# Gated linear attention and a bilinear feed-forward on one core: chunks 2 to 5 in blocks of 64 tokens, with a new order of the work

## The chip, the core and the metric

The kernel runs on one core of a Trainium2 chip. The core has TensorE (PE, matrix products, written to PSUM), VectorE (DVE), ScalarE (ACT), GpSimd (POOL) and SyncE (SP, which here issues transfers). They run side by side, each through its own list of instructions in order, and wait for one another by semaphores. Times are device microseconds (us) of one execution; the measure is the median of several.

## What is computed

Inputs are q, k, v and alpha, each 4 batches x 8 heads x 768 tokens x 48, in float32. A state of 48 x 48 per batch and head is carried over the tokens; its output y, put together over the heads to 3072 tokens x 384, goes through a feed-forward layer with two branches that are multiplied.

```python
for t in range(S):
    state = alpha[:, :, t, :, None] * state + np.einsum('bhd,bhe->bhde', k[:, :, t], v[:, :, t])
    y[:, :, t] = np.einsum('bhd,bhde->bhe', q[:, :, t], state)
x = y.transpose(0, 2, 1, 3).reshape(B * S, H * D)
out = (x @ w_a) * (x @ w_b) @ w_out          # 384 -> 1536 -> 384
```

## The kernel before, in words

**Chunks.** The work is six chunks. A chunk is 256 tokens of two batches (u = 0 and 1) with all 8 heads; chunks 2s and 2s+1 take the tokens from 256 s on, for batches 0, 1 and 2, 3. Partition p holds tokens 2p and 2p+1 (rank r = 0, 1), so partitions 0 to 63 are the first 128 tokens (frame g = 0) and 64 to 127 the second (g = 1). The state at the start of a chunk is in `S0`, that between its frames in `Sm`.

**What is done to a chunk.** `ln` takes the logarithm of alpha on ScalarE (L548); `l2` adds the pairs (L556); a product with a triangle of ones gives cumulative sums (`A`, `B`, `A2`; `AQ` for chunks 2 to 5, which needs two transfers `sw` that swap the frames' halves, L603, and the splits `R` on VectorE, L614); `E` takes their exponentials both ways on ScalarE (L658), `ra` the exponential of the second rank (L636). `lv`, `mk` and `mq` scale k and q by them (L643, L669) into `QKp`. `C`/`Ce` (TensorE and a copy) or `T` (a transposing transfer on SyncE, L722) turn `QKp` to `kqT`. Then come four kinds of small products on 64x64 quarters of TensorE's array:

- scores `D` (L777): keys by queries, within a frame and for each rank of the key, 64 x 128;
- the state products `K` (L748), 64 rows deep, 48 columns wide, and the update `k` on VectorE (L762 to L766);
- `SB`, `SA` (L801): queries by the state at the frame's start, the part carried in;
- `Y` (L801): masked scores by values, the inner part, into the same PSUM banks.

The scores are masked on VectorE from PSUM (`M`, L782) or copied by ScalarE and masked afterwards (`Mc`, L786, and `Mm`, L790). `v` copies the values into a padded tile (L734, L736). `X` puts the result into `xT` (L836, L838). The feed-forward follows: for each of 12 slices f of the hidden width, `a f` and `b f` (L855) are three products each, over 512 columns (`*`, the whole chunk) or 256 (one u); `as` copies the first branch out on ScalarE (L861), `pr` multiplies it with the second on VectorE (L869); `o m h` (L877) makes an output block of 128 tokens in two halves of six products, `ot` copies it out (L892, L894), `st` stores it.

**The order.** It is written by hand in the string `PROGRAM`: each entry is chunk, operation, arguments, the last of them a PSUM bank (0 to 7) or an engine (V, S, P, Y for VectorE, ScalarE, GpSimd, SyncE). Each engine gets its instructions in just that order, and the feed-forward of one chunk is woven into the attention part of the next. `a 6 * 3` is slice 6 of the first branch for the whole chunk in bank 3. A bank that is written again waits until its last reader is done: for `a`, the `as` on ScalarE; for `b`, the `pr` on VectorE. `dr` and `dl` carry the chunk's decay through memory into `bl`. `c1a` loads ScalarE's function table that has both Ln and Exp:

```python
    def const_table():
        nc.scalar.preload_act_table_set("natural_log_exp_and_others")
```

It is the fifth entry of the string, ahead of all activations.

Of the kernel before, what the change touches and what calls it, by code (L numbers as in the profile page):

```python
# [17 lines left out]
0: cz 0 q V; cs 0 m P; ld a 0b Y; c1; c1a; cs 0 0 P; cz 0 v V; ld a 0a Y; ln 0b; cu; fill 5 2; ld k 0b Y; ld q 0b Y; cu2 P; cus; cm 0; cz 1 q V; B 0b 0; ld q 0a Y  # L18
0: ld v 0 P; ld k 0a Y; ld a 1 P; ln 0a; ld q 1 P; ci; ld k 1 P; E 0b b; B 0a 3; E 0b i; W b 0 256; ld v 1 P; E 0a b; dk 0 0; mq 0b V; mk 0b V; E 0a i; C 0 1 5
0: mq 0a V; mk 0a V; cz 0 b P; fill 3 1; cm 1; Ce 0 1 V; C 0 0 1; W a 0 256; de 0; v 0 V; Ce 0 0 V; D 0 1 6; K 0 0 3; k 0 0 V; SB 0 2; W a 256 768; c3 V  # L20
0: M 0 1; ln 1; D 0 0 0; W b 256 768; Mc 0 0; B 1a 4
1: ld a 1 P
0: E 1a b
1: ld a 0 P
0: Mm 0 0 V; W a 768 1536; cz 1 b P; B 1b 0; E 1a i; E 1b i; cs 1 0 P; mk 1a V; E 1b b; dk 1 5; W b 768 1536; mq 1a V; Y 0; v 1 S; C 1 0 1; mq 1b V; mk 1b V
0: de 1; SA 0; Ce 1 0 V; C 1 1 6; X 0 S; Ce 1 1 V; K 1 0 0; D 1 0 4; a 0 0 3
1: ld k 0 P
0: Mc 1 0
1: ld q 0 P
0: k 1 0 V; D 1 1 1; M 1 1; a 1 0 7  # L30
1: ld v 0 P
0: a 5 0 6
1: ld q 1 P
0: Mm 1 0 V; a 3 0 5; as 1 0; as 0 0; Wo 0 6; b 0 0 7; as 5 0; c2 P; pr 0 0; SB 1 1; b 1 0 0; a 2 0 6; b 2 0 3; a 4 0 4; pr 1 0; as 2 0; b 5 0 0; pr 2 0
0: pr 5 0
1: ld k 1 P
0: as 3 0
1: ln 1
0: SA 1; Y 1
1: l2 1 V  # L40
0: K 1 1 0; K 0 1 3; k 1 1 V; X 1 S; as 4 0; b 4 0 6; b 3 0 5
1: ln 0
0: b 5 1 2; pr 3 0; a 4 1 4; a 5 1 0; a 1 1 7
1: l2 0 V
0: k 0 1 V; as 4 1; pr 4 0; b 1 1 5; as 5 1; b 2 1 1; b 4 1 0; a 6 * 4
1: H 0 S
0: Wo 6 12; as 1 1
1: H 1 S
0: pr 5 1; b 3 1 6; a 3 1 3; pr 4 1; a 11 * 0; a 8 * 2; a 2 1 7; pr 1 1; as 3 1
2: ld a * P  # L50
1: L 1 V; L 0 V
0: pr 3 1; as 6 *; as 8 *
1: ra 0
0: as 2 1; b 6 * 6
1: lv 0 q P
0: pr 6 *; b 8 * 5; b 11 * 4
1: A2 0 7
0: a 7 * 3
1: ld v 1 P
0: as 11 *; a 9 * 6; a 0 1 2  # L60
1: lv 0 k V; E 0 b; ra 1
0: pr 8 *
1: E 0 i
0: pr 2 1; b 9 * 0
1: A2 1 5
0: b 0 1 1; a 10 * 7; as 0 1; pr 11 *; as 9 *
1: E 1 b; mq 0 V
0: as 7 *; cz 1 v P; cs 1 m P
2: ld k * P
0: b 7 * 4; b 10 * 2  # L70
1: E 1 i; mk 0 V; lv 1 q V; C 0 1 6; mq 1 V
0: pr 9 *
1: Ce 0 1 S; C 0 0 3; dk * 0
0: pr 0 1; pr 7 *
2: ld v * P
1: v 0 V; D 0 1 5; K 0 0 1
0: as 10 *
1: K 0 1 4; de *; Ce 0 0 S; Mc 0 1; k 0 0 V
0: o 3 0 7; o 1 0 0; pr 10 *
1: lv 1 k V  # L80
2: ld q * P
1: mk 1 V; k 0 1 V; D 0 0 5; SB 0 1
2: ln *
1: M 0 0
0: o 0 0 3
1: Mm 0 1 V
0: o 0 1 -
1: C 1 1 4; Ce 1 1 V
0: o 3 1 -; ot 0 V
1: v 1 V; C 1 0 4  # L90
0: o 1 1 -
2: lv 0 k P; l2 * V
1: Ce 1 0 S; Y 0; K 1 0 5; K 1 1 6
2: sw Y
1: k 1 0 V; SA 0; D 1 0 3; X 0 S
0: o 2 0 5
1: k 1 1 V
0: ot 3 S; ot 1 V
2: ra 0
1: M 1 0; a 3 0 1; a 1 0 2; as 3 0; as 1 0; b 1 0 0  # L100
2: ra 1
1: a 11 0 7; b 3 0 6
3: ld a * P
1: a 5 0 2
0: o 2 1 -
1: pr 1 0; as 5 0
2: R 0
1: D 1 1 3; pr 3 0
2: lv 1 k P; R 1
0: ot 2 S  # L110
1: b 5 0 2; b 11 0 0; b 4 0 6; pr 5 0; a 4 0 1; Mc 1 1; as 11 0; Mm 1 1 V
2: v 0 V; AQ 4
1: as 4 0; pr 11 0; SB 1 2; a 2 0 1; a 10 0 7
3: ld v * P
4: ld a * P
1: b 10 0 0; pr 4 0
2: E 0 b
1: as 2 0; b 2 0 1; as 10 0
2: lv 1 q V; E 1 b; E 1 i
1: pr 10 0  # L120
2: lv 0 q V
1: SA 1; Y 1
2: E 0 i
1: pr 2 0; X 1 S; a 7 0 7; a 0 0 4; a 6 0 1
2: mk 1 V
1: as 6 0; b 6 0 5
2: dr
1: b 7 0 3
2: mq 1 V
1: as 7 0; a 0 1 2; a 8 0 0; b 0 0 7; pr 6 0; pr 7 0; as 0 0; as 8 0; pr 0 0; b 8 0 6; as 0 1  # L130
3: ln *
1: a 9 0 3
2: T 1
1: pr 8 0; b 0 1 4; pr 0 1; a 5 1 7; a 2 1 0; b 2 1 2
2: mq 0 V; dl
1: a 11 1 5; a 4 1 6; b 8 1 1; as 2 1; as 9 0; as 11 1; b 11 1 4; pr 2 1
2: v 1 V; mk 0 V
1: as 4 1; b 9 0 5
2: T 0
1: pr 9 0; b 4 1 3; a 6 1 6; a 9 1 2; b 9 1 0; as 5 1; b 3 1 5  # L140
0: st 1 Y
1: pr 4 1; pr 11 1
3: l2 * V
1: a 3 1 7; as 9 1; as 3 1
3: ra 0
1: b 5 1 3; pr 5 1; a 1 1 2; b 1 1 4; pr 9 1; a 8 1 7; pr 3 1
2: K * 0 0
1: as 6 1
0: st 0 Y; st 3 Y
3: sw Y  # L150
1: as 1 1; as 8 1
3: ra 1
2: D 1 0 5
0: st 2 Y
2: D 1 1 2
1: pr 1 1
2: M 1 1; Mc 1 0
1: b 6 1 4; pr 6 1; o 2 0 7; a 7 1 6
2: k * 0 V
3: ld k * Y; ld q * Y  # L160
1: a 10 1 2; as 10 1; as 7 1
5: ld k * Y
1: b 7 1 3; b 10 1 5; pr 10 1; o 2 1 -; pr 7 1; pr 8 1
2: Mm 1 0 V; SB 1 5; K * 1 3
4: ln *
1: ot 2 S
2: D 0 0 0
1: o 0 0 4; o 3 0 7
2: k * 1 V; Mc 0 0; SB 0 2
3: R 0; lv 0 q P  # L170
2: D 0 1 0
1: o 3 1 -
2: Y 1
3: R 1
2: Mc 0 1; Mm 0 1 V; Mm 0 0 V
3: lv 0 k V; AQ 0
2: SA 1
3: E 1 b; E 0 i
2: SA 0; Y 0; X 0 S
1: o 0 1 -  # L180
2: X 1 V
3: E 0 b
2: b 6 * 2; a 6 * 3
4: l2 * V
1: ot 0 S
3: E 1 i
2: as 6 *; a 2 * 6; a 1 * 4; b 7 * 5; a 5 * 0
4: sw Y
3: dr
2: b 1 * 3  # L190
3: mk 0 V
1: ot 3 V
2: as 1 *; as 2 *; b 8 * 1; a 8 * 7
3: mq 0 V; lv 1 q P
2: pr 6 *; b 2 * 6
3: lv 1 k P
4: ld q * Y
3: T 0
1: st 3 Y
4: ra 0  # L200
2: as 8 *; pr 1 *
3: mk 1 V
2: as 5 *
3: v 0 S
4: R 0
3: mq 1 V
2: pr 8 *
1: st 2 Y
3: T 1
2: a 7 * 2; pr 2 *; b 3 * 7; a 4 * 3; b 5 * 0; b 9 * 1; as 7 *; b 0 * 4; a 3 * 6; a 9 * 2; pr 7 *  # L210
4: R 1
2: pr 5 *; as 3 *
1: o 1 0 5
3: v 1 V
2: a 0 * 6; as 9 *; as 0 *
3: dl
1: o 1 1 -; st 0 Y
5: ld a * Y
2: pr 9 *; pr 3 *; as 4 *; pr 0 *
1: ot 1 V  # L220
4: ld k * Y
2: b 4 * 6; a 10 * 0
3: K * 0 1
5: ld q * Y
2: pr 4 *
3: D 0 0 4; M 0 0
2: b 10 * 3; a 11 * 6; b 11 * 7; as 10 *
3: k * 0 V
2: o 3 0 4; as 11 *; pr 10 *; pr 11 *
3: D 1 1 0; D 1 0 2; K * 1 5; k * 1 V; Mc 1 0; Mc 1 1  # L230
4: ra 1
2: o 0 0 7; o 0 1 -
3: SB 0 2
2: ot 0 S
3: SB 1 5; D 0 1 0
5: lv 1 k V
3: Mm 1 1 V
5: ln *
2: o 2 0 7
3: M 0 1; Mm 1 0 V  # L240
2: o 2 1 -; ot 2 V
4: AQ 0
3: SA 1
4: lv 1 q P; lv 0 q P; lv 1 k P
3: SA 0; Y 0
# [12 lines left out]
3: a 8 * 5
4: E 0 i; lv 0 k P
3: a 1 * 1; a 5 * 3  # L260
4: mq 0 V
1: st 1 Y
3: as 8 *; as 5 *; a 0 * 7
5: ld v * P; ra 1
3: b 8 * 2; a 9 * 6; a 3 * 3
5: lv 1 q P; lv 0 q V
4: mq 1 V; mk 0 V
3: b 5 * 0; pr 8 *; pr 5 *; b 3 * 5
5: lv 0 k P
3: b 9 * 4; as 9 *  # L270
4: mk 1 V; T 0; dr
3: a 4 * 6; a 2 * 2; as 3 *; as 1 *; b 2 * 1
5: R 0
3: pr 9 *; b 1 * 3
4: T 1
3: b 0 * 4; b 6 * 0
4: v 0 V
3: pr 3 *; pr 1 *; as 2 *
4: dl
2: st 0 Y  # L280
3: pr 2 *; as 4 *; as 0 *
4: v 1 S
3: b 4 * 5
4: D 0 0 2; Mc 0 0
3: a 11 * 1; pr 0 *; pr 4 *; a 6 * 6; as 11 *; a 7 * 7; as 6 *; as 7 *
4: D 1 1 4
3: pr 6 *
5: R 1
4: D 0 1 1; K * 0 3; Mc 0 1; k * 0 V; D 1 0 6; Mc 1 1
3: a 10 * 0; b 11 * 1  # L290
2: o 1 0 2
3: pr 11 *
4: Mm 0 0 V; Mc 1 0
# [72 lines left out]
4: pr 2 *; pr 9 *
3: st 3 Y; st 2 Y; st 1 Y
# [30 lines left out]
def kernel(  # L398
# [443 lines left out]
    def us_of(w):  # L842
        return FULL if w == "*" else HALVES[int(w)]
# [186 lines left out]
```

## Time and profile before

| | |
|---|---|
| Runs, us | 197.16, 196.88, 197.66 (median 197.16) |
| Profiled execution: span, us | 194.9; the page gives no other time of it, 2.3 under the median |
| TensorE busy, us | 188.1 |
| VectorE, ScalarE, GpSimd busy, us | 133.5, 106.7, 48.6 |
| Feed-forward products L855: 324 of 512, 216 of 256 columns, busy us | 81.0, 31.2 |
| Output products L877: 276 of 384 columns, busy us | 49.7 |
| Scores, state, carried and inner products: count | 384, 320, 240, 576 |
| TensorE's granted clock | full in all slices |

Busy times of TensorE overlap, because products are pipelined; the chain of waits in order of time gives the pace. A line of the groups names line, engine, operation, result and sources, shapes and count, then busy time and mean ns, then idle time before and what ended it. A line of the timeline or the chain begins with the start and the duration in us.

### The profile page before, as it was taken

The page shows a single profiled execution, that of the slowest core. Times are in us where ns is not written, and L with a number is a line of the kernel's source. Part 1 is how long each engine was busy: PE and PEld are TensorE (multiplying, and loading weights), DVE is VectorE, ACT ScalarE, POOL GpSimd, SP SyncE. Part 2 cuts the span into 40 slices and gives each one's busy share as a digit, 9 for nine tenths or more (in the row PEclk, how much of TensorE's full clock was granted, in tenths as well). Part 3 has the DMA queues.
Part 4 walks back from the last instruction along what each step waited for, and adds up shares of the span by engine and source line. Part 5 has one row for each costly group of instructions (what it writes and reads, how often), then busy time and mean ns, then how long its engine had stood idle before and what let it go on. Part 6 is the DMA issues. An engine that isn't in the chain of part 4 may idle for free.

```text
span 194.9 us, 6070 instructions
## 1 busy us (share of the span) xinstructions
PE 188.1 (97%) x2612; PEld 117.9 (60%) x2612; DVE 133.5 (69%) x224; ACT 106.7 (55%) x195; POOL 48.6 (25%) x67
## 2 busy tenths in 40 slices
PE   5989999999979999999999999999999999999993
PEld 2887875667658876644466644556455644455662
DVE  4477897986789989889888779689372816432311
ACT  4367677655668676644428655971394443632211
POOL 7999535901900000170005840000000000000000
PEclk9999999999999999999999999999999999999999
DMA  5999999999993799949999697501873100000314
GB/s 137 274 216 227 238 255 232 251 272 240 247 240 90 117 252 266 247 92 268 153 253 257 69 213 150 99 0 45 150 152 119 45 3 0 0 0 3 121 55 147
DMA packets 63258, 30.19 MB, mean 155 GB/s; under 512 B 53840, under 2 KB 61408, under 8 KB 63232
## 3 DMA queue, kind: packets, MB, share of 16 engines
q0 software_dynamic: 18432, 13.37, 39.1%
q1 hardware_dynamic: 44656, 16.34, 37.6%
q8 instruction: 20, 0.33, 0.7%
q10 hardware_dynamic: 144, 0.10, 0.2%
q14 instruction: 6, 0.05, 0.1%
HBM read 25.98 MB, written 4.74 MB: 158 GB/s over the span
## 4 chain that ended last, share of the span: by engine, by line
PE 90%; DMA 5%; DVE 2%; ACT 0%; issue 0%; SPq 0%; DVEq 0%
PE psum L855 47%; PE psum L877 22%; PE psum L801 7%; PE psum L777 3%; DMA l<-l 3%; PE psum L748 2%; PE psum L711 2%; PE psum L583 2%; DMA a_t<-in_alpha_dram 1%; PE psum L584 1%; PE psum L691 1%; PE psum L624 1%; PE psum L888 1%; DVE kqT L719 1%; DVE lh L614 0%; DVE l L556 0%
## 5 line engine op out<-in xcount | busy, mean ns | idle before, releaser
L855 PE MATMUL psum<-xT,wb_t 128*128 128x512 bf16 (+1 forms) x270 | 56.1, 337 | 1.2 <-DVE prod L869 1.1
L855 PE MATMUL psum<-xT,wa_t 128*128 128x512 bf16 (+1 forms) x270 | 55.6, 337 | 0.0
L877 PE MATMUL psum<-wo_t,prod 128*128 128x384 bf16 x276 | 49.7, 326 | 0.0
L855 PEld LDWEIGHTS <-wb_t 128*128 128x128 bf16 x270 | 25.8, 98 | 21.3 <-issue 1.8
L855 PEld LDWEIGHTS <-wa_t 128*128 128x128 bf16 x270 | 25.8, 98 | 19.6 <-issue 0.2
L877 PEld LDWEIGHTS <-prod 128*128 128x128 bf16 x276 | 25.8, 98 | 17.6 <-issue 0.3
L643 POOL TENSOR_TENSOR q_t<-q_t,ra 128x384 f32<-128x384 f32 x6 | 7.1, 1188 | 50.5 <-ACT xT L836 28.5
L786 ACT ACTIVATE m<-psum 128x1024 bf16<-128x1024 f32 x16 | 15.9, 1022 | 5.3 <-PE psum L777 5.2
L892 ACT ACTIVATE ot<-psum 128x384 f32<-128x384 f32 (+1 forms) x17 | 7.9, 472 | 15.9 <-PE psum L877 12.7
L548 ACT ACTIVATE la<-a_t 128x1536 f32<-128x1536 f32 (+2 forms) x9 | 9.5, 1056 | 5.0 <-DMA a_t<-in_alpha_dram 4.9
L782 DVE TENSOR_TENSOR m<-psum,mask 128x1024 bf16<-128x1024 f32 x8 | 9.8, 1221 | 2.7 <-PE psum L777 2.0
L790 DVE TENSOR_TENSOR m<-m,mask 128x1024 bf16<-128x1024 bf16 x16 | 10.5, 685 | 1.3 <-ACT m L786 1.3
L836 ACT ACTIVATE xT<-psum 128x768 bf16<-128x768 f32 x9 | 7.2, 810 | 6.1 <-PE psum L801 5.8
L894 DVE COPY ot<-psum 128x384 f32<-128x384 f32 x8 | 4.4, 550 | 8.7 <-PE psum L877 8.7
L669 DVE TENSOR_TENSOR QKp<-q_t,beta 128x768 bf16<-128x768 f32 x10 | 9.8, 984 | 0.7 <-ACT beta L658 0.6
L669 DVE TENSOR_TENSOR QKp<-k_t,invb 128x768 bf16<-128x768 f32 x10 | 10.2, 1031 | 0.0
L801 PE MATMUL psum<-m,vx 64*64 64x128 bf16 x576 | 10.1, 217 | 0.0
L777 PE MATMUL psum<-kqT 64*64 64x128 bf16 x384 | 9.9, 220 | 0.0
L643 POOL TENSOR_TENSOR k_t<-k_t,a_t 128x384 f32<-128x384 f32 x6 | 7.2, 1194 | 9.1 <-DMA k_t<-in_k_dram 9.1
L801 PEld LDWEIGHTS <-vx 64*64 64x64 bf16 x576 | 8.8, 107 | 0.7 <-issue 0.6
L541 POOL DMA_DIRECT2D v_t<-in_v_dram x8 | 8.6, 1073 | 0.2 <-issue 0.2
L777 PEld LDWEIGHTS <-kqT 64*64 64x64 bf16 x384 | 6.8, 106 | 3.0 <-issue 1.9
(267 smaller groups left out, 280.3 us busy)
## 6 DMA issues: line engine op xcount, KB each, us to landing
out_dram<-ot SPq DMA_DIRECT2D x23, 192.0 KB, 2.5
a_t<-in_alpha_dram POOLq DMA_DIRECT2D x3, 768.0 KB, 9.0
k_t<-in_k_dram SPq DMA_DIRECT2D x3, 768.0 KB, 9.1
q_t<-in_q_dram SPq DMA_DIRECT2D x3, 768.0 KB, 9.7
v_t<-in_v_dram POOLq DMA_DIRECT2D x4, 384.0 KB, 7.6
a_t<-in_alpha_dram POOLq DMA_DIRECT2D x3, 384.0 KB, 9.5
q_t<-in_q_dram POOLq DMA_DIRECT2D x3, 384.0 KB, 13.9
k_t<-in_k_dram POOLq DMA_DIRECT2D x3, 384.0 KB, 13.8
```

What stands on the lines that cost most here:

```text
L541: eng.dma_start(out=t[:, us, hs].rearrange("p b h r d -> p (b h) (r d)"), in_=src[ch.b0 + us.start:ch.b0 + us.stop, hs, ch.s * 2 * C:(ch.s ...
L548: nc.scalar.activation(out=ch.la[:, us, hs].rearrange("p b h r d -> p (b h r d)"), in_=ch.a[:, us, hs].rearrange("p b h r d -> p (b h r d) ...
L643: eng.tensor_mul(x, x, by)
L669: eng.tensor_mul(QKp[ch.c % 2][:, u, j, :, hs, :D], src[:, u, hs].rearrange("p h r d -> p r h d"), f)
L777: nc.tensor.matmul(s2[g * HC:(g + 1) * HC, r, p, rk, :], lhsT=ch.kqT[u][rs, 1, rk, 2 * h + p, g * HC:(g + 1) * HC], rhs=queriesT(ch, u, 2 ...
L782: nc.vector.tensor_mul(m.rearrange("p r a k s -> p (r a) (k s)"), ch.s2[u, h].rearrange("p r a k s -> p (r a) (k s)"), maskn(4))
L786: nc.scalar.activation(out=m.rearrange("p r a k s -> p (r a) (k s)"), in_=ch.s2[u, h].rearrange("p r a k s -> p (r a) (k s)"), func=AF.Copy)
L790: eng.tensor_mul(x, x, maskn(4))
L801: nc.tensor.matmul(y[c * DP:(c + 1) * DP, g, j // 2 * C:(j // 2 + 1) * C], lhsT=lhsT, rhs=rhs, start=(g, c) not in begun, stop=False, skip ...
L855: nc.tensor.matmul(p, lhsT=(wa_t, wb_t)[w][:, kk, f * 128:(f + 1) * 128], rhs=ch.xT[:, kk, us, :], start=(kk == 0), stop=(kk == KT - 1))
L877: nc.tensor.matmul(op, lhsT=ch.prod[:, f, at:at + C], rhs=wo_t[:, f, :], start=(f == 0), stop=(f == NFF - 1))
L892: nc.scalar.activation(out=o_, in_=i_, func=AF.Copy)
```

## The change

Chunks 0 and 1 are computed as before. In chunks 2 to 5 a frame is split into two blocks of 32 partitions (64 tokens, q = 0 and 1):

- `keys2` (`kk`) copies the turned keys into 32-partition blocks with both ranks beside each other; `scores2` (`D2`) multiplies 64 key tokens by 32 partitions of queries: 64 columns per product, half the scores of before. One mask of 32 partitions (`mask2`) serves them all; a chunk has two score tiles of 1024 columns instead of four.
- A third and fourth state, `Sq`, stands in the middle of each frame, undecayed: the state at the frame's start plus the first block's products. `state_pe2` (`K2`) makes the state products by blocks, as tiles of 32 rows by 64 columns, straight from the loaded values; `state2` (`k2`) adds them up.
- `carried2` (`SB2`, `SA2`) uses a state for each block, `inner2` (`Y2`) the blocked scores, `evac2` (`X2`) puts results to `xT` in the new order of tokens, and `pr` reads that order.
- `values` (`vt`) puts the values into the padded tile by eight transfers within SBUF on SyncE, where a copy by VectorE or ScalarE stood.

The string `PROGRAM` is new throughout: the orders, banks and engines of all chunks. GpSimd gets `l2` of chunks 2, 3 and 5 and most of the `kk`. `c1a` stands in chunk 5. The core of the diff:

```diff
 PROGRAM = """
-0: cz 0 q V; cs 0 m P; ld a 0b Y; c1; c1a; cs 0 0 P; cz 0 v V; ld a 0a Y; ln 0b; cu; fill 5 2; ld k 0b Y; ld q 0b Y; cu2 P; cus; cm 0; cz 1 q V; B 0b 0; ld q 0a Y
...
+0: ld a 0b Y; c1; fill 5 4; cz 0 q V; cm 1; ci; ln 0b; cu; cu2 P; cus; ld q 0b Y; ld a 0a Y; ln 0a; B 0b 1; E 0b b; E 0b i; mq 0b V; ld k 0b Y; mk 0b V
+0: B 0a 3; E 0a i; E 0a b; dk 0 7; cz 0 b P; de 0; C 0 1 2; Ce 0 1 S; ld v 0 P; ld a 1 P; W a 256 768; cs 1 q P; cz 1 b P; ld q 1 P; cs 0 m P; ld v 1 P
+0: ln 1; fill 3 6; ld k 0a Y; ld q 0a Y; mk 0a V; mq 0a V; C 0 0 0; v 0 V; K 0 0 6; D 0 1 4; Ce 0 0 V; D 0 0 0; Mc 0 0; k 0 0 V; SB 0 2; dk 1 7; de 1; cm 0
+0: cz 0 v V; M 0 1; Mm 0 0 V; c3 V; B 1a 6; E 1a b; mq 1a V; v 1 V; SA 0; Y 0; X 0 S; ld k 1 P; E 1a i; mk 1a V; B 1b 4; E 1b i; mk 1b V; E 1b b; mq 1b V
+0: a 5 0 7; as 5 0; a 3 0 1; a 2 0 6; as 3 0; as 2 0; C 1 0 5; Ce 1 0 V; C 1 1 7; W b 256 768; b 3 0 3; b 5 0 2; pr 3 0; K 1 0 1; k 1 0 V; D 1 0 4; pr 5 0
...
+2: K2 4157; k2 0 V; dl; k2 1 V; k2 2 V
...
+2: kk 1 P; D2 1 5; Mc2 1; T 0; kk 0 P
+3: sw Y; R 0
...
+2: D2 0 0; Mc2 0; Mm2 0 V
+3: ld q * Y; lv 1 q P
+2: SB2 1 2; SB2 0 6
...
+2: SA2 0; SA2 1; Mm2 1 V; vt; Y2 1; X2 1 V
+3: E 1 i; E 1 b; mq 1 V
...
+2: Y2 0; X2 0 S
+1: o 0 1 -; ot 0 S
+3: E 0 i; lv 0 q V
+1: o 3 1 -; ot 3 V
+3: ld v * P
+2: a 6 * 2; b 9 * 3; a 9 * 5
+4: ln *; ra 0; l2 * V
+3: mq 0 V
+2: a 7 * 0; b 7 * 1; as 9 *; as 6 *; as 7 *; pr 7 *; b 6 * 5
...
+3: vt; mk 1 V
+2: pr 6 *
+3: dl; T 1
...
+3: a 5 * 3; as 10 *; b 3 * 2; pr 3 *; b 10 * 4; as 5 *; pr 5 *
+5: ln *; l2 * P; lv 1 k P; sw Y
+3: pr 10 *; a 8 * 3; a 4 * 2
 5: ra 0
+3: as 8 *; a 2 * 5; b 8 * 1; as 2 *; pr 8 *; b 2 * 3; a 6 * 4; a 11 * 1; pr 2 *; as 4 *; as 1 *; as 11 *; pr 1 *; b 4 * 3
...
+0: c1a
+4: vt; Y2 0
+5: vt
...
+    def keys2(ch, u, eng):
...
+        ch.kk[u] = t = wk.tile([C, P2, 4, HC], BF16, name="kk", bufs=2)
+        o_ = t.rearrange("p a b (r s) -> p r (a b) s", r=2)
+        i_ = ch.kqT[u][:, 1].rearrange("p r a (b s) -> p r (a b) s", s=QC)
+        for r in range(2):
...
+                eng.tensor_copy(o_[:, r], i_[:, r])
+    def scores2(ch, u, tag):
+        ch.s2[u] = s2 = wide(tag).rearrange("p r (g a s) -> p r g a s", g=2, a=P2)
+        for p in range(P2):
+            for g in range(2):
+                for q in range(2):
+                    for r in range(2):
+                        b = 2 * g + q
+                        nc.tensor.matmul(s2[half(q), r, g, p, :], lhsT=ch.kk[u][half(r), p, b], rhs=block(ch, u, 0, p, b, half(r)), start=True, stop=True)
...
+    def masked_in_place2(ch, u, eng):
+        x = ch.m[u].rearrange("p r g a s -> p (r g a) s")
+        eng.tensor_mul(x, x, mask2n(16))
+    def values(ch):
+        ch.vt = vxs[ch.c % 2].rearrange("p g b h e -> p g (b h) e")
+        for r in range(2):
+            for g in range(2):
+                for q in range(2):
+                    at, of = q * HC + r * QC, (2 * g + q) * QC
+                    nc.sync.dma_start(out=ch.vt[at:at + QC, g, :, :D], in_=ch.v[of:of + QC, :, :, r].rearrange("p b h e -> p (b h) e"))
...
+    def carried2(ch, u, g, crossed):
...
+                    st = Sq[g][half(r), u] if q else Sm[ch.c % 2][half(r), u] if g else S0[ch.s % 2][half(r), ch.b0 + u]
+                    out_mm2(ch, u, q, g, h, j, st[:, at:at + DP], block(ch, u, 0, h // 2, 2 * g + q, half(r)))
+    def inner2(ch, u):
...
+                    for q in range(2):
+                        out_mm2(ch, u, q, g, h, j, vx[half(q), g, u, at:at + DP], ch.m[u][half(q), h % 2, g, h // 2, :])
+    def evac2(ch, u, eng):
...
+    def state_pe2(ch, tags):
...
+                    for b in range(len(tags)):
+                        bs = slice(b * QC, (b + 1) * QC)
+                        for r in range(2):
+                            nc.tensor.matmul(ch.kv[b][half(r), e:e + D], lhsT=QKp[i][bs, u, 1, rk, 2 * p + r, :], rhs=ch.v[bs, u, 2 * p + r, rk, :],
+                                             start=(rk == 0), stop=(rk == 1), tile_position=(b * QC, r * HC))
+    def state2(ch, b, eng):
...
+        if b == 0 and ch.s == 0:
+            nc.vector.tensor_copy(mid, x)
+        elif b % 2 == 0:
+            nc.vector.tensor_add(mid, x, ends[g])
+        else:
...
+            nc.vector.tensor_add(tmp, x, mid)
+            eng.tensor_mul(ends[g + 1], tmp, bl)
```

## The prediction

> **What bounds the kernel now.** I read the page's first part, then the chain that ended last, then the groups by shape, then the waits, and last the timelines of TensorE, ScalarE and SyncE.
>
> ```profile
> PE 188.1 (97%) x2612; PEld 117.9 (60%) x2612; DVE 133.5 (69%) x224; ACT 106.7 (55%) x195; POOL 48.6 (25%) x67
> PE 90%; DMA 5%; DVE 2%; ACT 0%; issue 0%; SPq 0%; DVEq 0%
> ```
> TensorE is busy through 97% of the span and is 90% of the chain. A busy share says nothing of speed, so I read the chain in order of time:
>
> ```profile
> 48.08 5.95 DMA l<-l
> 54.12 0.96 DVE lh L614
> 102.10 0.50 PE psum L748 x32
> 104.66 0.46 PE psum L801 x24
> 132.18 1.80 PE psum L801 x120
> 155.97 15.64 PE psum L855 x72
> ```
> 72 feed-forward products of 512 columns take 15.64 us, 0.217 each, with nothing between them. From 24 to 120 small products (L801) the time grows by 1.34 us: 14.0 ns each, and 0.12 us for coming into this array mode and out of it. State products (L748), 48 columns wide, take 0.50/32 = 15.6 ns although they stream fewer columns. The timeline shows why 14:
>
> ```profile
> 104.67 0.22 PE L801 MATMUL psum<-kqT,Sm 64*64 64x128 bf16 x1
> 104.67 0.22 PE L801 MATMUL psum<-kqT,S 64*64 64x128 bf16 x1
> 104.67 0.22 PE L801 MATMUL psum<-kqT,Sm 64*64 64x128 bf16 x1
> 104.68 0.22 PE L801 MATMUL psum<-kqT,S 64*64 64x128 bf16 x1
> 104.72 0.22 PE L801 MATMUL psum<-kqT,Sm 64*64 64x128 bf16 x1
> ```
> Four products on the four 64x64 tiles start within 10 ns; the next four start 55 ns later. So a round of four costs what 128 columns cost. L748 uses two tiles at a time (one half of the rows), in rounds of 2 x 15.6 = 31 ns. After 12 us TensorE waits for some 1.7 us in all (1.1 of it in one wait at 54 us, behind the chain from the `l<-l` transfer; the rest in small bits, read from gaps between starts). It is bound by its own work, and ScalarE, at 55%, has slack.
>
> ```profile
> L461 ACT ACT_TABLE_LOAD x1 | 1.3, 1283 | 0.7 <-PEq L1014 0.7
> L548 ACT ACTIVATE la<-a_t 128x1536 f32<-128x1536 f32 x4 | 5.9, 1483 | 2.7 <-DMA a_t<-in_alpha_dram 2.7
> L636 ACT ACTIVATE ra<-la 128x384 f32<-128x384 f32 x10 | 5.2, 520 | 0.0
> 85.82 4.65 SPq L722 DMA_TRANSPOSE kqT<-QKp  x1
> 98.70 4.16 SPq L541 DMA_DIRECT2D q_t<-in_q_dram  x1
> 111.16 1.17 SPq L603 DMA_DIRECT2D l<-l  x2
> ```
> One table load, at the start, serves the whole program. [...]
>
> The profiled span is 194.9 us; the median of the runs is 197.16. I make the sum on the span and add the 2.3 us between them.
>
> **The change, part by part.**
>
> Small products of chunks 2 to 5. Before: 256 scores, 384 within the chunk, 192 carried, each at 14.0 ns: 832 x 14.0 = 11.65 us; 192 state products at 15.6: 3.0 us. After: 256 scores, 384 inner and 384 carried (two states a chunk more), all 64 columns wide: 1024; and 448 state products on 32-row tiles. Price of a 64-column product: half of 14.0 = 7.0 at best, 14.0 if columns aren't what counts. I take 8.0, a quarter of L748's 31 ns round, which is nearest (64 weight columns, 48 streamed): 8.2 us. State product: eight tiles in one 31 ns round is 4.0; no better than now, 15.6. I take 4.0 because four starts already fit into 10 ns: 1.8 us. Together 10.0 against 14.65: **-4.65**. Ends: -5.7, and 14.3 + 7.0 - 14.65 = +6.7. Changes of array mode fall from 60 to 53, at 0.1 each: **-0.7**. The feed-forward part (540 + 276 + 24 products) is unchanged in number and shape.
>
> Table loads. `c1a` moves from the program's start to chunk 5. The built order then has 15 loads instead of 1: ScalarE swaps tables at each turn from Ln to Exp and back. 14 x 1.283 = 18.0 us more on ScalarE. Against that it loses 4 of 16 score evictions (4.1 us) and 4 value casts (3.4) and gains small copies: about 118 busy of 195, 61%. It doesn't become the bound on average, so a load costs only where TensorE's next bank waits for ScalarE. I walk those places.
>
> (a) Chunk 2's feed-forward, T = end of its last `Y2`. TensorE: `o 0 1`, `o 3 1` 12 x 0.163 = 1.95, then `a 6, b 9, a 9, a 7, b 7` at 0.65: at T+5.2 it wants bank 5 for `b 6`, which `as 9` must empty. ScalarE: two 384-column pieces of xT (0.47 each, as L892's) to T+1.1; ot (after `o 0 1`) T+1.7; invb T+2.2; load, la, load, ra: +1.28+1.48+1.28+0.52 = T+6.75; `as 9` T+7.35. Stall 2.1; without the loads 4.8, none.
> (b) Chunk 3's: `ln *` and `ra 0` of chunk 5 stand between `as 5` and `as 8`. From the end of `a 5`: TensorE reaches `b 2` (bank 3, held by `a 8`) after six products, 3.9; ScalarE 0.75 + 4.56 + 0.6 = 5.9. Stall 2.0; none without.
> (c) xT behind `load, ln` three times (chunk 0 second half, chunk 1 both): after the chunk's last inner product TensorE has one output product (6 x 0.163 = 1.0) and at most a bit more as cover, ScalarE still has the rest of load and la (1.28 + 1.48, less what ran before that end) and xT (0.81) to do: counted along the order, TensorE is 0.4, 0.6 and 0.85 late, which the loads alone make.
> (d) Chunk 2's cumulative sums: Ln is 1.3 later, and l2, the transfer and both `R` follow: 1.3 late.
> Sum 7.25; I take **+7**. Ends: 0, if buffers and run-ahead cover all; 18.0, all on the path.
>
> [...]
>
> Transfers. `vt` puts eight SBUF-to-SBUF transfers a chunk on SyncE: 8 x 0.59 (the `l<-l` row) = 4.7 us at best. In chunk 2 they stand behind `T 0` (1.6 to 4.65), two `l` (1.2) and a q load (1.6 to 4.2), and land 2.5 to 5 later: 11.6 to 19.8 us after `T 0` is issued. TensorE gets to `Y2 1` about 11 us after the same point (5.2 landing, 2.4 for `kk`, 3.3 of own work), so it waits 0 to 8; I take 1.5, near the uncrowded issue. Chunk 3's `vt` stands ahead of `dl` and `T 1`, so what is queued behind it is `kk 1` and the scores: 0 to 5, I take 1.5. Chunks 4 and 5: 0.5. Queued behind on SyncE besides: k and q loads and stores, all with many us of slack.
>
> GpSimd gets `l2` of three chunks and 12 of 16 `kk` copies. 768 columns there are twice the 1.19 us of L643, against 1.0 on VectorE: 1.4 longer in chain (d), of which 0.5 shows. Sum of transfers and GpSimd: **+4** (0 to 13). The 1.7 us of stalls of before stand at places of the old order: **-1.7**.
>
> VectorE loses 4 first masks (1.22) and 4 second (0.69), gains the mid-frame sums (0.55 each); it stays near 69% and costs nothing beside TensorE, as long as `pr` keeps up as it does now.
>
> Start. k 1 and the second half of the weights come later in GpSimd's queue; the first feed-forward product comes at about 16.3 instead of 18.6, but then the transposes wait for k 1 until about 17.8. Counting products done, both are even at 25 us: **0** (-1 to +1.5). The tail is the same: one store after the last half product.
>
> Sum: 194.9 - 4.65 - 0.7 + 7 + 4 - 1.7 = 198.85; with 2.3 around it **201.1**.
>
> **Rivals.**
> Faster: the loads are covered. For it: ScalarE idles 45%, and an `as` of 0.6 for every 1.3 us of products catches up fast. Against it: walks (a) and (b), where the order names the bank. With loads at 1.5 and transfers at 2.5: 197.2 - 5.35 - 1.7 + 4.0 = **194.1**. It decides when loads and transfers together stay under 7.05 us.
> [...]
> SyncE piles up: in chunks 2 and 3 the issues run at 4 us, as the transposes and loads do at 82 to 102 us: transfers 10 instead of 4: **207**. Against it: 96-byte pieces are few bytes.
> The 64-column products cost 14 and state products 15.6: +6.7 for -4.65, part of it under the stalls: about **209**. Against it: four starts in 10 ns.
> The change does less than it says: excluded, the built order has the products.
>
> **How the numbers follow.** Forecast 0.42, covered loads 0.24, double swap 0.11, SyncE 0.12, dear products 0.03, and 0.08 for a balance within 0.5% of 197.16, about what a measurement of this kernel tells from no change. Predicted: 201. The forecast's own range is 198.3 to 204. Range 193.5 to 207.5: down through the covered case with -5.7 for the products, up to the SyncE and double-swap cases. Faster 0.24, same 0.08, slower 0.68 (0.42 + 0.11 + 0.12 + 0.03).
>
> **What would show it.** 15 ACT_TABLE_LOAD rows of about 1.28 us; whether the activation after each starts at once (swap price). Chain pieces of 48 or 96 products (the new inner and carried lines) at 8 ns, and 128 state products in 0.5 us. TensorE waits before `b 6` of chunk 2 and `b 2` of chunk 3, ended by ScalarE; before `Y2` of chunk 2 and `D2` of chunk 3, ended by a transfer. The forecast is wrong if TensorE's idle after 25 us is under 5 us, or if the new products don't get cheaper.

## The result, and the profile after

The changed kernel takes 219.24 us (median of 217.18, 218.27, 220.20 and 222.27), the kernel before 197.18 beside it: 1.109 times as long, interval 1.1025 to 1.1162. The profiled execution is that of 218.27 us, with a span of 216.5 against 194.9. The sign of the forecast is right; its size, 201.1, misses by 18 us, and the time lies far outside the range. Medians are of all runs of a kernel; ratios and intervals are of its runs within 1.5% of the fastest.

From the page of the changed kernel: the busy times, the clock that TensorE was granted in 40 slices (tenths), the transfers that bring instructions (packets, MB, share of the engines), and the chain that ended last.

```profile
PE 193.0 (89%) x3060; PEld 119.6 (55%) x3060; DVE 130.0 (60%) x227; ACT 118.3 (55%) x203; POOL 63.1 (29%) x96
...
PEclk9988999999999999999999999699999999999999
...
q8 instruction: 24, 0.39, 0.8%
...
PE 44%; ACT 4%; DMA 4%; issue 3%; ACTq 0%
```

TensorE's share falls from 97% to 89%: of the 21.6 us more, 16.7 are idle (23.5 against 6.8), and 4.9 are longer busy times. ScalarE has 118 us, as reckoned, and isn't the bound. New are an "issue" of 3% in the chain, where TensorE waits for nothing that the profile shows, and two dips in the row of clocks. The chain in order of time (start and duration in us):

```profile
99.12 10.52 PE psum L885 x48
...
136.26 5.73 PE psum L885 x18
142.00 1.05 PE psum L853 x96
...
149.01 0.26 PE psum L775 x32
...
153.19 2.16 issue
...
174.79 0.51 PE psum L806 x48
```

The feed-forward products run at 0.219 each as before (10.52/48), but at 136 us 18 of them take 5.73, 0.318 each on average. The new scores (L775, 64 columns) take 8.1 ns each and the new carried products (L806) about 10 with a change of mode: as forecast. The state products on 32-row tiles (L853) take 10.9 here, not 4.0.

TensorE's waits, by its own lines (total, times, longest):

```profile
PE psum L806 <- issue: 4.3, 3, 2.2
PE psum L806 <- DMA vx<-v_t: 2.1, 2, 1.9
PE psum L885 <- ACT as__2661 L891: 2.0, 1, 2.0
PE psum L885 <- ACT xT L744: 2.0, 3, 1.0
PE psum L885 <- ACT as__1977 L891: 1.9, 1, 1.9
PE psum L908 <- issue: 1.2, 1, 1.2
...
PE psum L537 <- DVE ll L507: 1.0, 1, 1.0
```

The gaps between the starts of neighbouring products, where they are over 0.25 us beyond the usual step, sum to 24.3 us, against 2.9 before. (This is more than the idle time, because a product counts as busy until its own end.) `as__1977` and `as__2661` are the two places of walks (a) and (b): banks 5 and 3, which `as 9` of chunk 2 and `as 8` of chunk 3 must empty. ScalarE's timeline at (a):

```profile
93.93 1.28 ACT L456 ACT_TABLE_LOAD   x1
95.22 1.48 ACT L456 ACTIVATE la<-a_t 128x1536 f32<-128x1536 f32 x1
96.77 1.28 ACT L544 ACT_TABLE_LOAD   x1
98.06 0.52 ACT L544 ACTIVATE ra<-la 128x384 f32<-128x384 f32 x1
98.49 0.58 ACT L891 ACTIVATE as__1977<-psum 128x512 bf16<-128x512 f32 x1
```

The logarithms follow 1.29 us after the start of their load, and so does `ra`; the loads themselves start 0.03 and 0.07 us after the end of the activation ahead of them (93.42 + 0.48, 95.22 + 1.48). So a swap here costs its record of 1.28 us and nothing more; a second wait with each load, the double swap of the forecast's chances, does not show in these rows.

The "issue" waits are four: at 78.9, 84.6, 123.6 and 155.3 us, 6.0 us in all with the usual step taken off. The last one on the timeline, in the midst of 24 carried products, all of whose operands are long there:

```profile
152.99 0.19 PE L806 MATMUL psum<-kqT,S 64*64 64x64 bf16 x1
153.00 0.19 PE L806 MATMUL psum<-kqT,Sq 64*64 64x64 bf16 x1
155.35 0.19 PE L806 MATMUL psum<-kqT,S 64*64 64x64 bf16 x1 [2.16 <-issue]
155.36 0.21 PE L806 MATMUL psum<-kqT,Sq 64*64 64x64 bf16 x1
```

Counted through TensorE's list (a weight load and a product are two instructions; a float32 product four, since the 8 of L491 have 16 records of each kind), the four products stand at these places. The transfers are those of the queue q8: 24 packets of 16384 bytes. That they bring TensorE's list, 256 instructions in each, is an estimate from counts and not shown directly: 24 packets come for a list of 6139 records (256 for each), 20 for the 5230 of before (262), and the places fit.

```
wait at    length   place in list   place mod 256   a packet's transfer began
 78.93      1.36        2239             191         2.40 us earlier
 84.61      0.92        2495             191         2.67
123.64      1.45        3774             190         2.36
155.35      2.29        4798             190         2.44
```

Counted more simply, by all records of TensorE's list that had started before the wait (its semaphore instructions too, its opening drain not), each of the four stands at exactly 192 of 256.

So the suspicion after the result: TensorE waits for its own instructions, where 256 of them pass sooner than a packet comes. The small products, at 4 to 5 ns an instruction (8.1 to 10.9 ns for the two of a product), pass quickly; a 512-column product takes 217 ns for its two. The quickest 256 instructions between two such places took 1.6 us in the changed kernel, 4.9 in the one before.

The clock: stretches of the timeline around 136 us (TensorE's busy time and count first, then those of the other engines, the granted clock, transfers).

```profile
133.40:136.80 3.40, 1.38 (x7) 0.58 (x6) 0.56 (x1) 3.31 (x6) 2.76 (x2) 1.00 0.58 134
136.80:140.20 3.40, 3.40 (x10) 1.16 (x8) 1.88 (x5) 1.44 (x3) 1.49 (x3) 0.53 0.81 134
```

The wait of 2.0 us for `as__2661` leaves TensorE busy for 41% of one stretch, and through the next 3.4 us the granted clock is 0.53.

### The profile page after: what moved, and what is told of

The parts are those of the page before. It is cut to its first block, busy times and chain, and to the rows that moved or that the text cites. A ratio compares the mean times of both kernels' runs of the same rounds, so it can differ in the third digit from the quotient of the medians.

```text
span 216.5 us, 7098 instructions
## 1 busy us (share of the span) xinstructions
PE 193.0 (89%) x3060; PEld 119.6 (55%) x3060; DVE 130.0 (60%) x227; ACT 118.3 (55%) x203; POOL 63.1 (29%) x96
## 4 chain that ended last, share of the span: by engine, by line
PE 44%; ACT 4%; DMA 4%; issue 3%; ACTq 0%
PE psum L885 25%; PE psum L908 13%; DMA kqT<-QKp 4%; PE psum L806 3%; ACT la L456 1%; PE psum L853 1%; PE psum L919 1%; PE psum L775 1%; ACT L456 1%; PE psum L532 1%; ACT ra L544 0%; ACT kk L764 0%; ACT as__2642 L891 0%; ACT as__1977 L891 0%; ACT as__2661 L891 0%
## 5 line engine op out<-in xcount | busy, mean ns | idle before, releaser
L885 PE MATMUL psum<-xT,wb_t 128*128 128x512 bf16 (+1 forms) x270 | 57.9, 339 | 6.3 <-ACT as__2661 L891 2.0
L885 PE MATMUL psum<-xT,wa_t 128*128 128x512 bf16 (+1 forms) x270 | 57.7, 342 | 0.2 <-ACT xT L744 0.2
L766 POOL COPY kk<-kqT 128x512 bf16<-128x512 bf16 x12 | 8.1, 699 | 48.1 <-DMA kqT<-QKp 48.1
L464 POOL TENSOR_TENSOR l<-la 128x768 f32<-128x768 f32 x3 | 5.4, 1815 | 30.9 <-DMA row<-beta 17.3
L788 ACT ACTIVATE m<-psum 128x1024 bf16<-128x1024 f32 x8 | 8.2, 1023 | 8.9 <-PE psum L775 8.9
L925 DVE COPY ot<-psum 128x384 f32<-128x384 f32 (+1 forms) x12 | 6.3, 537 | 9.4 <-PE psum L908 9.3
L840 DVE CAST xT<-psum 128x384 bf16<-128x384 f32 x8 | 4.1, 552 | 10.3 <-PE psum L806 10.3
L566 ACT ACTIVATE invb<-psum 128x384 f32<-128x384 f32 x10 | 4.9, 492 | 6.3 <-PE psum L532 5.0
L806 PEld LDWEIGHTS <-Sq 64*64 64x64 bf16 x192 | 4.5, 107 | 5.8 <-issue 5.2
L806 PE MATMUL psum<-kqT,S 64*64 64x64 bf16 x96 | 4.6, 195 | 3.5 <-issue 3.5
```

What stands on the lines that cost most here:

```text
L464: eng.tensor_add(ch.l2[:, us, hs].rearrange("p b h d -> p (b h) d"), x[:, :, 0, :], x[:, :, 1, :])
L766: eng.tensor_copy(o_[:, r], i_[:, r])
L788: nc.scalar.activation(out=o_, in_=i_, func=AF.Copy)
L806: nc.tensor.matmul(y[half(c), q, at:at + HC], lhsT=lhsT, rhs=rhs, start=(q, c) not in begun, stop=False, skip_group_check=True)
L885: nc.tensor.matmul(p, lhsT=(wa_t, wb_t)[w][:, kk, f * 128:(f + 1) * 128], rhs=ch.xT[:, kk, us, :], start=(kk == 0), stop=(kk == KT - 1))
L925: eng.tensor_copy(o_, i_)
```

## The experiments

All times in us; "clock" is the mean granted clock of each run, in the order of the runs.

| kernel | runs | ratio to before (interval) | clock |
|---|---|---|---|
| changed | 218.27, 222.27, 217.18, 220.20 | 1.109 (1.103 to 1.116) | .982 .968 .984 .983 |
| e1 table first | 210.57, 214.17, 212.73, 215.34 | 1.073 (1.066 to 1.080) | .991 .992 .981 .984 |
| e2 before, table late | 203.13, 205.04, 203.54, 201.31 | 1.026 (1.019 to 1.033) | 1.0 .992 1.0 1.0 |
| e3 changed, list shifted 128 | 224.39, 223.21, 227.75, 226.06 | 1.138 (1.131 to 1.145) | .954 .961 .962 .970 |
| e4 changed, wait filled | 218.78, 215.83, 221.03, 218.27 | 1.103 (1.096 to 1.111) | .976 .992 .961 .984 |
| e5 before, list shifted 128 | 206.78, 204.51, 203.96, 209.42 | 1.039 (1.032 to 1.047) | .992 1.0 1.0 .984 |
| e6 e1, turns first | 214.27, 213.33, 215.52, 215.75 | 1.089 (1.082 to 1.096) | .984 .984 .973 .976 |
| e7 e1, half states | 213.88, 214.05 | 1.084 (1.081 to 1.088) | .982 .983 |
| e8 e1, turns and swap first | 211.14, 217.18, 211.99, 211.41 | 1.073 (1.067 to 1.079) | .984 .976 .991 .984 |
| e9 e1, no value transfers | 208.49, 207.16, 207.26, 205.94 | 1.049 (1.042 to 1.056) | .992 .992 .991 1.0 |
| e10 e8, list shifted 48 | 211.62, 209.20, 213.88, 214.34 | 1.067 (1.057 to 1.078) | .984 .984 .975 .967 |
| e11 changed, no value transfers | 218.67, 212.55, 218.20, 221.48 | none | .969 1.0 .976 .961 |
| e12 e9, list shifted 60 | 203.85, 203.87, 207.02, 203.08 | 1.034 (1.029 to 1.038) | .992 .992 .991 .992 |
| e13 e9, list shifted 160 | 211.93, 210.83, 214.20, 213.18 | 1.076 (1.070 to 1.083) | .981 .984 .976 .984 |

e11 has no ratio, because its runs spread by 9 us. That spread is the clock: (1 - clock) times the span is 6.7, 0, 5.2 and 8.6 us of e11's four runs, and with it taken off they are 212.0, 212.6, 213.0 and 212.9. I call such a time "at full clock" below; it is worked out, and it takes off a little too much where TensorE stood idle in a slow stretch.

**e1, e2: the table loads**

```diff
-0: ld a 0b Y; c1; fill 5 4;
+0: ld a 0b Y; c1; c1a; fill 5 4;
...
-0: c1a
```

> The changed kernel with the one preload of ScalarE's table (c1a) put back into the first line, so that 1 table load should be left of 15; nothing else is moved. Theory A (the loads stretch short waits of TensorE, each by up to its 1.28 us): the waits that end in ScalarE go, which are 1.15 us at 27 to 28 us, 0.9 at 52, about 1.0 at 61, 1.2 at 68, 2.1 at 97 (b 6 behind as 9), 1.1 at 117, 2.2 at 134 (b 2 behind as 8) and some 1.5 in the start, together 9 to 11 us, and with the last of them the half-clock stretch at 137 us (1.7 us): 219.2 becomes 207 to 210. Rival B (the loads are covered, and the excess comes from waits for transfers, instructions and tiles): less than 3 us goes, 216 to 219. [...]

1 load is left, and 213.45 us: 5.8 less by the medians, 7.2 by the ratios; at full clock 215.0 becomes 210.4, 4.5 less. The waits of both walks are gone, as are those at 28, 37 and 53 us and 1.4 in the start, some 10 us. But two others have grown. TensorE's waits in e1:

```profile
PE psum L805 <- DMA kqT<-QKp: 3.4, 1, 3.4
...
PE psum L774 <- POOL kk L765: 1.7, 1, 1.7
...
PE psum L774 <- DVE Sq L864: 0.9, 1, 0.9
```

They are `SB2 0` and `D2 1` of chunk 3, behind `T 0` and `T 1`: the loads had hidden SyncE's lateness (0.4 us was to be seen of it). Theory A is right on the waits and, by the medians, over 3 us too high on the gain.

> The kernel before with its preload of the table moved to where the changed kernel has it, behind the first exponential of chunk 5; 1 table load becomes 15, and nothing else changes. This prices the loads in the old order. If they cost what theory A says of the changed order (8 to 12 us), 197.2 becomes 205 to 209 and waits for ScalarE of 1 to 2 us appear in TensorE's row, ahead of chunk 1 and in the FF blocks that share their stretch with logarithms and exponentials. If the old order covers them (rival B), it stays below 200. [...]

203.34, so the loads alone cost the old order 6.3 us by the medians, 5.1 by the ratio (interval 1.9 to 3.3%). They cost it in small coin: e2's list of waits has eight for ScalarE of 0.3 to 0.8 us, none over 1, where the changed order puts two of 2.0 behind one bank. The size is between both theories.

**e3, e5: where the packets of instructions end**

```diff
+    def pad(n, i):
+        for _ in range(n):
+            nc.tensor.matmul(bank(i)[:32, :2], lhsT=wz[:32, :32], rhs=wz[:32, :2], start=True, stop=True)
...
-c1; fill 5 4; cz
+c1; fill 5 4; pad 64 4; cz
```

In e5 it is `pad 64 2`, behind `fill 5 2` of the old order.

> The changed kernel with 64 products of 32x32 by 2 columns on the zero tile behind fill 5 4 in the start, in a stretch where TensorE waits for logarithms: 128 more instructions of TensorE, and a cost of at most 0.5 us there. Theory F (TensorE waits for its own instructions, which come in packets of 16384 bytes, so one wait at most per 256 instructions, at index 190 of 256): the four waits at 78.9, 84.6, 123.6 and 155.3 us (1.36, 0.92, 1.45 and 2.29 us) leave these products, and those that there are then lie again at index 190 to 191 of 256, so 128 instructions earlier in the order, where such a place falls into a run of small products; the sum of them is between 1.5 and 8 us, so the time is 214 to 222. Rival G (these four waits are for a bank, a tile or a mode of the array that the trace does not name): they stay at the same products, with the same lengths, and the time is 219 to 220.

```profile
PE psum L810 <- issue: 5.6, 2, 4.7
...
PE psum L889 <- issue: 1.6, 1, 1.6
```

The four waits have left their products. New ones stand at 29.98 (1.8), 117.94 (0.73), 124.13 (1.10) and 130.15 us (4.79); by the count of all records each is at 192 of 256, and each ends 2.3 to 2.7 us after the start of a packet. They are 8.4 us in all (the last three are the 6.6 that the expectation of e10 goes by); the one at 29.98 us stands where the changed kernel had two waits for ScalarE (1.2). Theory F holds, G is out. The time, 225.2, is above the upper bound that I gave: the start takes 1.0 more, and the clock is low for longer (0.954 by 222.6 us is 10 us lost, against 4).

> The kernel before with the same 64 small products (128 instructions of TensorE) behind fill 5 2 in the start; they take up to 1 us there, as in the run of the changed kernel with them. The kernel before had no wait at index 190 of 256. Theory F1 (such waits come with the change, because its small products are twice as many and half as long, and 256 instructions pass in less time than a packet of instructions needs): moved by half a packet the old order has still less than 1 us of them, 197.5 to 199. Theory F2 (the old order only had its packets' ends in good places): 2 to 6 us of waits at index 190 or 191 appear ahead of its small products, and the time is 200 to 204.

```profile
PE psum L805 <- issue: 2.6, 1, 2.6
...
PE psum L781 <- issue: 1.5, 1, 1.5
```

205.64, and the old order has such waits too: the larger (2.8 us beyond the usual step) among products of chunk 2, the other (1.7) among those of chunk 0. This trace lacks some records; with those put back from the list of before, both are at 192. With 1.5 us more in the start and, in this run, 1.6 of halved clock, that is most of the 8.4 us (7.7 by the ratio). So F2 is nearer: the kernel before wasn't free of this by its larger products alone, but also by where its packets end.

**e4: is the clock's dip due to the wait ahead of it?**

```diff
-as 2 *; pr 8 *; b 2 * 3;
+as 2 *; pr 8 *; fill 9 7; b 2 * 3;
```

> The changed kernel with 9 products of 512 columns on the zero tile, into bank 7 that is free there, ahead of b 2 * 3 in chunk 3, where TensorE otherwise waits 2.2 us for ScalarE: 9 by 214 ns is 1.93 us, inside that wait. Theory D (the half-clock stretch of 3.4 us at 137 us follows from the idle TensorE): the stretch at 0.5 goes from the row of granted clocks there, and the 18 products of 427 ns run at 214: 1.7 us less than 219.2, so about 217.5. Rival E (the stretch comes for another reason, such as the load before it): the stretch stays, and the time is 219 to 219.5.

The dip at 137 us is gone from the row of clocks, but in this run another stands at 114.6 us, so the mean (218.53) doesn't move beyond its spread. The clock's changes keep a grid of 3.41 us stretches: the dips are 3.41 or 6.83 us long, and those of the changed kernel at 14.10 and 136.98 us lie 36 stretches apart. On this grid, TensorE was busy for 41% of the stretch before the dip at 137 us; 17% in e1, 26, 41 and 44% in e3. But a stretch of 44% brought none in the changed kernel and in e4, nor did one of 49% in the changed kernel, and ahead of e4's dip it was 63%. The profiles of the changed kernel, e3 and e11 have the wait and a dip right behind it; that of e4 has neither. So the wait made the dip at 137 us, as far as one profile of each can show it; a threshold isn't shown.

**e6, e8: SyncE's order in chunk 3**

```diff
-3: vt; mk 1 V
+3: mk 1 V
...
-3: dl; T 1
-1: st 2 Y
+3: dl; T 1
...
-3: mk 0 V
+3: mk 0 V; T 0; vt
+1: st 2 Y
```

> The changed kernel with the table loaded first (213.45 us), and in chunk 3 SyncE's order changed: both transposing transfers T 1 and T 0 go as soon as their sources are written, ahead of the eight value transfers vt, of the store st 2 and of the loads and the swap of chunk 4. Theory A (with the loads gone SyncE's row in chunk 3 sets the time): the waits of 1.8 us (D2 1 for kk, for T 1) and 3.5 us (SB2 0, for T 0) go, and with the 3.5 us the half-clock stretch behind it (1.7 us): 213.45 becomes 206 to 208. Rival B (the transfers only change places: the values or chunk 4's rows become late by as much): waits of 2 to 5 us appear at Y2 of chunk 3 or at AQ of chunk 4, and the time is 211 to 214.

214.9: no gain. The two waits went, and this one came:

```profile
PE psum L805 <- DVE prod L899: 8.2, 1, 8.2
```

SyncE issued `vt` at 101 to 107 us and chunk 4's swap only at 109; `R 0`, which waits for it, stood ahead of `pr 10` on VectorE, and `pr 10` held bank 5 for `SB2 1`. Rival B, with another victim than it named. e8 puts the load of q and the swap ahead of `vt` as well, and `R 0` behind `k2 3`:

```diff
-4: ld q * Y; lv 0 q P; ra 1; lv 1 q P
+4: ld q * Y; sw Y; lv 0 q P; ra 1; lv 1 q P
+3: vt
...
-4: sw Y; R 0
...
+4: R 0
```

> The changed kernel with the table loaded first (213.45 us), and in chunk 3 SyncE's order T 1, T 0, chunk 4's load of q and its swap sw, and only then the values vt and the store st 2; R 0 of chunk 4, which waits for the swap, stands behind pr 10 and k2 3 on VectorE. In the run with the transposing transfers alone moved ahead, the swap came late by 8 us, and R 0 held pr 10 and with it SB2 1. Theory A (what counts on SyncE is that nothing that TensorE or VectorE needs at once stands behind the eight value transfers, which Y2 needs 10 us later): the waits of 1.8 and 3.5 us and the 8.2 us of the last run are absent, and so is the half-clock stretch behind them: 206 to 208. Rival B (chunk 3's SyncE row is full, and something is late in any order): waits of 2 us and more appear at Y2 or AQ, 210 to 214.

211.7. All waits of over 0.4 us between 82 and 130 us are gone, but in chunk 4 TensorE now waits: for VectorE at 131.5 (`pr`) and 133 us (`k2`), for `kk` at 136 and for `Sq` at 139 (`DVE Sq L865: 2.8` in its list). It comes there 4 to 5 us sooner, ahead of chunk 4's turned keys, which SyncE issued at 122.0 and not at 124.1. So B again: the row that was full in chunk 3 is met in chunk 4.

**e7: what sets the price of a state product**

```diff
-nc.tensor.matmul(ch.kv[b][half(r), e:e + D], ..., rhs=ch.v[bs, u, 2 * p + r, rk, :],
+nc.tensor.matmul(ch.kv[b][half(r), e:e + D // 2], ..., rhs=ch.v[bs, u, 2 * p + r, rk, :D // 2],
```

> The changed kernel with the table loaded first, and the state products of chunks 2 to 5 with 24 columns in place of 48; the other half of each state is left out. As many instructions, half the columns. It settles what a 32x64 state product costs, 8.9 ns in the changed kernel where the forecast had 4.0. Theory I (each costs the issue of its weight load and itself, about 4.4 ns apiece, whatever its columns): they stay at 8 to 9 ns each. Theory P (each costs its columns, so many that fit beside each other): 4.4 to 5 ns each, and the 128 of chunk 3 take 0.6 us less. The time itself differs by less than 2 us from 213.45 in either case.

The 128 of chunk 3, first in e1, then in e7:

```profile
100.43 1.23 PE L852 MATMUL psum<-v_t,QKp 32*64 32x48 bf16 x128
```
```profile
104.92 1.33 PE L852 MATMUL psum<-v_t,QKp 32*64 32x24 bf16 x128
```

Half the columns save nothing; taking off the last product's own 0.2 us, it is 8.1 and 9.0 ns each. Theory P is out. That the issue of two instructions sets the price fits this, and the 8.1 ns of scores with 64 columns, but no run varied it by itself.

**e9, e11: the value transfers**

```diff
     def values(ch):
...
-        for r in range(2):
+        for r in range(0):
```

> The changed kernel with the table loaded first, in the order of the changed kernel, without the 32 value transfers of chunks 2 to 5: their small products read old values. It prices the reordering of values by transfers. Theory A (they cost by what stands behind them on SyncE): in chunk 3 T 1 and T 0 go 5 to 6 us earlier, the waits of 1.8 and 3.5 us and the half-clock stretch go, 213.45 becomes 206 to 208, with the waits for instructions as before. Rival B (the transposing transfers are late for another reason, the swap or the load of the DMA engines): less than 2 us, 211.5 to 213.5.

207.2, 6.2 less than e1 by the medians, 4.7 by the ratios and 4.5 at full clock, with none of the two waits of chunk 3. Theory A. Of what is left, "issue" is the largest part:

```profile
PE psum L805 <- issue: 4.6, 4, 2.6
...
PE psum L907 <- issue: 1.2, 1, 1.2
PE psum L884 <- issue: 0.9, 1, 0.9
```

> The changed kernel (219.2 us, the table loaded late, 15 loads) without the value transfers of chunks 2 to 5; the small products read old values. With the table first, leaving the transfers out gave 6.2 us (213.45 to 207.2). Theory A (loads and transfers cost side by side): 219.2 becomes 213. Theory B (behind the late loads the transfers are mostly covered, and all that they cost is the wait of 2.4 us at Y2 1 of chunk 2 and 1 us in chunk 3): 215.5 to 217.

218.4 as measured, 0.8 below the changed kernel; at full clock 212.6 against 215.0, 2.4 less. Theory B: with the loads late, most of what the transfers cost is behind waits for ScalarE, and either of the two can go with little gain.

**e10, e12, e13: the same work, packets elsewhere**

`pad 24`, `pad 30` and `pad 80` in the start, in e8 (first) and e9.

> The kernel with chunk 3's transposing transfers and chunk 4's swap ahead of the values, and 24 small products (48 instructions of TensorE) behind fill 5 4 in the start, at up to 0.4 us. By the pace of the changed kernel's trace, with a packet of instructions that must be asked for some 4 us ahead, the ends of packets would then fall where the waits for instructions sum to 2.9 us, not 4.0 (at a shift of 128: 5.2 to 6.8; there the changed kernel had 6.6 of them). Theory F: 0 to 2 us faster than the same kernel without the products, the waits again at index 190 or 191. Rival G (place does not matter): 0.4 us slower.

212.75 against 211.7, with spreads of 5 and 6 us: nothing can be told of the time. In the one profile the waits for instructions sum to 4.0 us, not 2.9, again at 192 by the count of all records (in that of e8 to 4.1): theory F has the places right here, but the fall that it forecast is not seen.

> The kernel with the table first and without value transfers (207.2 us, 7.6 us of waits at index 189 to 192 of 256 in its profile) with 30 small products (60 instructions) in the start, at up to 0.5 us. If each packet must be asked for 4.5 us ahead, the pace of that kernel's trace gives 7.9 us of waits as it stands and 4.7 to 5.0 shifted by 56 to 64. Theory F: waits at these places sum to about 5, and the time is 203.5 to 206. Rival G (places do not set them): 7 to 8 us again, 207 to 208.

> The same with 80 small products (160 instructions), at up to 1 us in the start. The same reckoning gives 11.6 us of waits at this shift. Theory F: about 11, and the time is 210 to 213. Rival G: 7 to 8 us of waits, 207.5 to 208.5.

203.86 and 212.56, both as theory F has it, and 8.7 us apart with the same products. TensorE's list, in e12:

```profile
PE psum L809 <- issue: 3.0, 2, 1.8
PE psum L712 <- issue: 2.0, 1, 2.0
```

and in e13:

```profile
PE psum L809 <- issue: 5.0, 3, 2.5
PE psum L911 <- issue: 2.7, 1, 2.7
...
PE psum L712 <- issue: 1.0, 1, 1.0
```

Beyond the usual step these are 5.4 us and 9.4, all at 192 by the count of all records; the reckoning said 4.7 to 5.0 and 11.6. Of the difference in time, 4.0 are these, 1.4 the longer start, and some 2 the lower clock of e13 (0.981 of 210.2 us, against 0.992 of 202.1); the rest of some 1.3 is not assigned. e12 is the best of the kernels with the new products, and it leaves the value transfers out; none beats the kernel before. With its 5.4 us of waits and 1.7 us of halved clock taken off, e12 would be near 196.8 by estimate, beside 196.9 of the kernel before.

The places are the strongest evidence. The new kernels have ten profiles with the whole list (changed, e1, e3, e4, e8 to e13). In them every wait of over 0.5 us beyond the usual step that is put down to "issue" stands at 192 of 256, wherever the shift has moved that place. The 256 instructions ahead of it had passed in 1.2 to 6.2 us; no stretch that took longer has such a wait, and not every quicker one does.

## Why the prediction was right in sign and wrong in size

*Loads, +7.* The walks are right: (a) 2.1 forecast, 2.07 measured; (b) 2.0 and 2.19; both at the bank named. (c) was 0.4, 0.6 and 0.85 us, and is 1.15, 0.91 and 1.20; the third is nearly as long without the loads (1.08, then for a `pr`), so it isn't theirs. (d) was 1.3; its place has two waits of 1.75 in all, 1.15 of which stand in e1 too. Not walked were `A2` of chunk 1 (1.4) and the start (1.4). The waits of the loads come to about 10 us; taking them away saves 4.5 to 7.2 in this order (e1), and adding them to the old one costs 5.1 to 6.3 (e2), since others stand behind them.

*Transfers, +4.* `Y2` of chunk 2 waits 2.4 (1.5 forecast). `D2` of chunk 3 did not wait for `T 1`, because the loads made TensorE late there; without them it does. Shown: 2.4 us in the changed kernel, 4.5 with the table first, at full clock. The mechanism held; what the sum had no term for is that the two costs cover each other. For an issue on SyncE the prediction took 0.59 to 4.65 us; in the trace of before three loads in a row, from 96.58 us on, took 0.40, 1.64 and 4.16, and no run shows what sets the time of an issue.

*Small products, -4.65, and changes of mode, -0.7.* This term is mis-sized. 64-column products cost 8.1 ns, as taken. But the state products cost 8.1 to 10.9, 128 of them 1.0 us and not 0.5, where I took 4.0 from "four starts fit into 10 ns"; in e7 half the columns saved nothing (9.0 ns, against 8.1). All steps of chunks 2 to 5, changes of mode in them: 768 at 10.7, 256 at 10.9 and 448 at 10.0 make 15.5 us; before, at that trace's averages, 576 at 16.3, 256 at 19.2 and 192 at 15.6 make 17.3. So -1.8 instead of -5.35.

*Not in the sum: the list of instructions, +6.0.* This is the step that failed most. I counted how many products there are and what each costs, but not that 1472 small products of two instructions pass at 4 to 5 ns an instruction, and that the list itself has to come in, here in 24 packets. e3, e12 and e13, where a shift alone made these waits 8.4, 5.4 and 9.4 us, show that it is a cause of its own. The sum and all its rivals put this term at nothing. The page had its row before the change, and I passed over it because its share is small:

```profile
q8 instruction: 20, 0.33, 0.7%
```

*Not in the sum: the clock, about +4.* The mean clock of 0.982 takes 3.9 of 216.5 us. Behind the wait of 2.0 us at 136 us the products ran at half the clock for 3.41 us; I took a wait for its own length.

*Start, 0.* Forecast even; it has nearly 2 us of waits for ScalarE more (1.4 of them by the loads), and a dip of the clock at 14 us.

Together: 6.0 + 4 + 3.5 (products) + some 3 (loads beyond 7) - 1 (transfers: 2.4, and 0.4 at `T 0`, for 4) + 2.5 (what is left, not assigned) is 18, the miss. This adds up waits of one trace; taken away one at a time, loads and transfers are worth less (e1, e11).

*The rivals.* Covered loads: out, by e1 and e2. Double swap (0.11, and a part of the range's upper bound): no run shows a second wait with a load; behind 13 of the changed kernel's 15 loads the activation started 1.29 to 1.30 us after the load did, behind the other two it waited for a transfer and a product. SyncE pile-up: it was there, hidden (e1, e6, e9). Dear products: right for the state products only.

## What to carry to other kernels

When a change doubles the number of small instructions, ask what brings them in: count the engine's list in packets, and look where 256 instructions pass quickly (here no wait of over 0.5 us stood behind a stretch of more than 6.2 us). Before a kernel is judged, shift its list by a few harmless instructions: here the same work gave 203.9 and 212.6 us, and the kernel before lost some 8 by a shift of 128, 1.5 of it in the start. Waits that share a stretch are not added up: here, with the loads away (e1), waits of 3.4 and 1.7 us for the transfers showed.

## What the runs showed of the hardware

By the estimate above, TensorE's instructions come here in packets of 16384 bytes and 256 instructions; it waited 0.3 to 4.8 us at the place 192 of some of them. Each of these waits ended 2.2 to 2.9 us after the start of a packet's transfer. The reckoning by pace gave 5.2 to 6.8 us for e3 (measured 8.4), 2.9 for e10 (4.0), 4.7 to 5.0 for e12 (5.4) and 11.6 for e13 (9.4), so it came within some 3 us. Its lead, 4 us for e10 and 4.5 for e12 and e13, is my assumption: no trace shows when a packet is asked for, and why the transfers begin when they do stays open.

In the changed kernel, from 0.7 us after the end of a wait of 2.0 us, TensorE's clock was at half for 3.41 us: busy for 41% of one stretch, it had 0.5 in the next, and the 18 products of 512 columns behind the wait took 0.318 us each on average. Behind the waits of 1.9 us that ended at 99.1 us and of 2.2 us that ended at 155.4 us, in the same trace, the clock stayed full.

A small product took 8.1 ns at 64 columns on 64x64 tiles (the changed kernel's scores) and 8.1 to 9.0 at 48 or 24 columns on 32x64 tiles (e1, e7): tiles of half the rows brought nothing.
